# Normalising the first token tile by halves, with its square sums added on GpSimd and the early weight conversions spaced out

## The chip, the cores and the metric

The kernel runs on one core of a Trainium2 chip. The metric is the device time of one execution in microseconds (us). The engines are TensorE (PE in the profile, its weight loads PEld), VectorE (DVE), ScalarE (ACT), GpSimd (POOL) and SyncE (SP), which issues all the DMA transfers of this kernel.

## The reference

Three layers run one after another on 4 x 576 = 2304 tokens of width 512, all in float32.

```python
scores = q @ k.T / 8                              # 4 batches, 8 heads of 64, 576 positions
x = (scores * gamma[h] ** (i - j) * (j <= i)) @ v # retention
rms = sqrt(mean(x * x, axis=-1) + 1e-6)
xn = x / rms * rms_g
g = xn @ w_gate                                   # 512 -> 1536
y = (g * sigmoid(g) * (xn @ w_val)) @ w_out       # 1536 -> 512
out = relu(y @ w_in) ** 2 @ w_out2                # 512 -> 2048 -> 512
```

## The kernel before

**Layout.** Activations lie transposed in `X`, channels on the partitions (4 blocks of 128) and tokens along the row. Retention is done in 16 pairs (4 batches x 4 pairs of heads). `scores(n, half)` multiplies q by k for chunks of 128 positions and masks the product on VectorE, `state(n)` builds the state between chunks (`R`), `outputs(n, half)` forms the output and writes it to `X`, `scale_v(n)` scales the values on ScalarE. The loop for `n` runs `scores(n, 0)`, `outputs(n-1, 0)`, `state(n)`, `scores(n, 1)`, `outputs(n-1, 1)`.

**Weights.** A weight piece is 128 x 512 numbers of 8 bytes. It is loaded into one of three staging buffers (`load_piece`), and `convert_piece` turns it into a main part and a rest, both of the type that TensorE multiplies (`w[:, 0]`, `w[:, 1]`): three ScalarE and four VectorE instructions. Activations are split the same way (`split_x`, tiles `xh` and `xl`), and each product is made of three (`mm3`). `halves(k)` adds k to a counter; each 2 in it convert one piece, and each conversion loads the piece that lies `cv["ahead"]` further on. `LOAD_W` names the loops at whose start `ahead` grows by one, `CONVERT_ALONE` the loops of the first eight at whose end conversions stand.

**The first token tile.** Tokens 0 to 511 are complete after pair 3. They are normalised in two groups of 256 tokens during the next pairs, by steps listed in `NORMS` under (loop, half): "squares" (ScalarE squares, then two additions that fold 4 blocks into one), "roots" (TensorE sums over partitions into bank `ssq`, then a reciprocal root of two VectorE and twelve GpSimd instructions), "scale" (TensorE spreads the roots into bank `rms`, VectorE scales `X`) and "split" (`xh`, `xl`). From loop 8 on (`FIRST` is 7), 20 blocks of the second layer's first product (`glu_gate`, `glu_val`, 12 products each) run between the pairs: `block()`. Before loop 8, `keep_warm` issues products of zeros into a bank `junk`, one call at each half of a loop.

**Order.** TensorE's and SyncE's instructions run in the order of the program text. A planner orders VectorE, ScalarE and GpSimd by its own estimate of when inputs are there; `tc.high_priority()` around the steps of `NORMS` raises them in it. All queues run in order on the chip. `CONVERT_BEHIND[cv["phase"]]` can bind a conversion behind the last ScalarE ("a") and VectorE ("d") instruction that the text has issued; in phases 0 and 1 it is free, in 2 and 3 it is bound to both.

Of the kernel before, what the change touches and what calls it, by code (L numbers as in the profile page):

```python
# [11 lines left out]
ALU = mybir.AluOpType  # L12
PSUM = bass.MemoryType.PSUM

P = 128
# [15 lines left out]
GRP = 256  # L31
NGV = 2 * NF1
# [4 lines left out]
NWB = NF1 - NKEPT // 2 - NWC  # L37
FIRST = 7
WARM = (8, 6, 5, 5)
WARM_PAIR = (1, 1)  # L40
NORMS = {
    (4, 0): [("squares", 0)], (4, 1): [("squares", 1)], (5, 1): [("roots", (0, 1))],
    (7, 0): [("scale", 0), ("split", 0)], (7, 1): [("scale", 1), ("split", 1)],
    (9, 0): [("squares", 2)], (10, 0): [("roots", (2,))], (11, 0): [("scale", 2)],
}
LOAD_W = (4, 5, 6)
CONVERT_ALONE = {5: 2, 6: 2, 7: 4}
CONVERT_BEHIND = ("", "", "ad", "ad")
RSQRT_MAGIC = float(0x5F3759DF)
I32 = mybir.dt.int32  # L50
# [5 lines left out]
def retention_then_glu_then_relu2(ctx: ExitStack, tc: tile.TileContext, qk, kv, w1, w2, g, cmask, cvs, cgi, cgc, cid, out):  # L56
    nc = tc.nc
# [14 lines left out]
    def bank(tag, name):  # L72
        return psum.tile([P, 512], F32, tag=tag, name=name)
# [5 lines left out]
    ones = const.tile([P, 1], F32, name="ones")  # L79
# [12 lines left out]
    last_on = {}  # L92
    cv = {"load": 0, "done": 0, "half": 0, "lim": 0, "load_lim": NP1, "phase": 0, "ahead": 0}
# [14 lines left out]
    def convert():  # L108
        i = cv["done"]
        if i not in raws or i >= cv["lim"]:  # L110
            return False
        raw = raws.pop(i)
        with ExitStack() as behind:
            for e in CONVERT_BEHIND[cv["phase"]]:
                behind.enter_context(tc.issue_after(last_on[e].ins))
            convert_piece(i, raw)
        cv["done"] += 1
        return True
# [21 lines left out]
    def halves(k):  # L140
        cv["half"] += k
        while cv["half"] >= 2 and convert():
            cv["half"] -= 2
        cv["half"] = min(cv["half"], 2)

    def need(n):
        while cv["done"] < n:
            assert convert()


    aside = wa.tile([P, 2, 512], F32, tag="w", name="aside")
    ident, sums = aside[:, 0, :P], aside[:, 1].rearrange("p (i n) -> p i n", i=2)
    cols_ = aside[:, 0, P:P + 12].rearrange("p (k n) -> p k n", k=3)
# [4 lines left out]
    alone = {"on": True}  # L158
# [34 lines left out]
    def keep_warm(k, new=False):  # L193
        if new:
            junk["t"] = bank("G", f"junk{len(junk)}")
        for _ in range(k):
            nc.tensor.matmul(junk["t"][:, :P], zero, zero, start=True, stop=True)
# [102 lines left out]
    def roots(y, z, ms, sums, aside=False):  # L300

        last_on["d"] = nc.vector.tensor_scalar(
            out=ms, in0=sums, scalar1=1.0 / DM, scalar2=1e-6, op0=ALU.mult, op1=ALU.add
        )
        last_on["d"] = nc.vector.tensor_scalar(
            out=y.bitcast(I32), in0=ms.bitcast(I32), scalar1=-0.5, scalar2=RSQRT_MAGIC, op0=ALU.mult, op1=ALU.add
        )
        for _ in range(3):
            if aside:
                nc.gpsimd.tensor_tensor(out=z, in0=y, in1=y, op=ALU.mult)  # L310
                nc.gpsimd.tensor_tensor(out=z, in0=z, in1=ms, op=ALU.mult)
                nc.gpsimd.tensor_scalar(out=z, in0=z, scalar1=-0.5, scalar2=1.5, op0=ALU.mult, op1=ALU.add)
                nc.gpsimd.tensor_tensor(out=y, in0=y, in1=z, op=ALU.mult)
                continue
            for o, a, c, op0, b, op1 in (
                (z, y, -0.5, ALU.mult, y, ALU.mult), (z, z, 1.0, ALU.mult, ms, ALU.mult), (y, z, 1.5, ALU.add, y, ALU.mult),
            ):
                last_on["d"] = nc.vector.scalar_tensor_tensor(out=o, in0=a, scalar=c, in1=b, op0=op0, op1=op1)

    def scale_x(i, rb):  # L320
        ts = slice(i * GRP, i * GRP + GRP)
        for k in range(KC):
            last_on["d"] = nc.vector.scalar_tensor_tensor(
                out=X[:, k, ts], in0=X[:, k, ts], scalar=gsb[:, k:k + 1], in1=rb, op0=ALU.mult, op1=ALU.mult
            )
# [17 lines left out]
    def beside(what, i):  # L343
        nb = GRP // P
        if what == "squares":
            sq = wa.tile([P, KC, GRP], F32, tag="w", name=f"sq{i}")
            last_on["a"] = nc.scalar.activation(out=sq, in_=X[:, :, i * GRP:i * GRP + GRP], func=AF.Square)
            last_on["d"] = nc.vector.tensor_tensor(out=sq[:, 0:2], in0=sq[:, 0:2], in1=sq[:, 2:4], op=ALU.add)
            last_on["d"] = nc.vector.tensor_tensor(out=sums[:, i % 2], in0=sq[:, 0], in1=sq[:, 1], op=ALU.add)
        elif what == "roots":  # L350
            pb = bank("V", f"ssq{i[0]}")
            for j in range(nb * len(i)):
                nc.tensor.matmul(
                    pb[:, j:j + 1], sums[:, i[j // nb] % 2, j % nb * P:j % nb * P + P], ones, start=True, stop=True
                )
            y, z, ms = (cols_[:, k, :nb * len(i)] for k in range(3))
            roots(y, z, ms, pb[:, :nb * len(i)], aside=True)
        elif what == "scale":
            rb = bank("V", f"rms{i}")[:, :GRP]
            for j in range(nb):  # L360
                at = i % 2 * nb + j
                nc.tensor.matmul(
                    rb[:, j * P:j * P + P], cols_[:, 0, at:at + 1].to_broadcast([P, P]), ident, start=True, stop=True
                )
            scale_x(i, rb)
        else:
            split_x(i * GRP, GRP, i * GRP)
# [126 lines left out]
    for n in range(1, NPAIR + 1):  # L494
        mixed = n > FIRST
        if n in LOAD_W:
            cv["ahead"] += 1
            load_ahead(cv["done"])
        if n == FIRST + 1:
            alone["on"] = False  # L500
            cv["phase"] = 1
        if n < NPAIR:
            scores(n, 0)
        if mixed:
            block()
        else:
            keep_warm(WARM_PAIR[0], True)
        outputs(n - 1, 0)
        stages(n, 0)
        if n < NPAIR:  # L510
            state(n)
            if n == NPAIR - 1:
                att_kv.close()
                wpool["c"] = ctx.enter_context(tc.tile_pool(name="wc", bufs=NWC, side="right", reuse_waits="tile"))
                cv["lim"] = NGV + NWC
                cv["load_lim"] = NP1
                load_ahead(cv["done"])
        if mixed:
            block()
        else:  # L520
            keep_warm(WARM_PAIR[1])
        if n < NPAIR:
            scores(n, 1)
        outputs(n - 1, 1)
        stages(n, 1)
        scale_v(n + 1)
        halves(CONVERT_ALONE[n] if n in CONVERT_ALONE else 2 * mixed)
    assert points["done"] == len(blocks)
    att.close()
    cv["phase"] = 2  # L530
# [180 lines left out]
```

## Time and profile before

| | |
|---|---|
| runs, median (lowest to highest) | 965.57 us (965.51 to 967.13) |
| profiled execution, time | 966.28 us |
| profiled execution, span from first to last instruction | 964.5 us |
| TensorE busy | 938.8 us (97%) |
| VectorE busy | 493.7 us (51%) |
| ScalarE busy | 339.7 us (35%) |
| GpSimd busy | 23.0 us (2%) |
| mean granted TensorE clock | 0.989 of full |

Of the profiled time, 1.78 us lies outside the span. TensorE's 25.7 us without work and the granted clock by stage are what the change can touch; the other engines matter where TensorE waits for them.

### The profile page before, as it was taken

To read this page: it belongs to the slowest core of one execution; us is meant where nothing else is said; L and a number is where in the kernel's file an instruction comes from. 1 tells how busy PE (TensorE), PEld (TensorE's weight loads), DVE (VectorE), ACT (ScalarE), POOL (GpSimd) and SP (SyncE) were. 2 spreads that over 40 slices of the span, in tenths; PEclk is the share of its full clock that TensorE was granted. 3 is DMA by queue.
4 is the path that set the end of the run, shared out by engine and by line. 5 is a ranking of instruction groups with operands and counts; after the bars stand their busy time and mean duration, and the time that the engine had idled before them with its cause. 6 is when DMAs were issued, how large, how long until landed. Compare 5 with 4: busy or idle time off the path is not lost.

```text
span 964.5 us, 12744 instructions
## 1 busy us (share of the span) xinstructions
PE 938.8 (97%) x5248; PEld 782.9 (81%) x5248; DVE 493.7 (51%) x917; ACT 339.7 (35%) x606; POOL 23.0 (2%) x44
## 2 busy tenths in 40 slices
PE   9859999899999999999999999999999999999998
PEld 8747776799988888888888888888888888888897
DVE  3777887677655424442587786632224222322332
ACT  2544452555231113111455565432223222322332
POOL 0100100002010000000000000000000000000000
PEclk9969999999999999999999999999999999999999
DMA  8844653231000000000044423001001000100010
GB/s 291 291 146 147 225 185 109 65 111 44 1 1 1 23 1 1 22 22 1 13 141 131 131 95 103 22 1 45 0 1 45 1 1 1 43 1 1 1 45 22
DMA packets 22554, 60.92 MB, mean 63 GB/s; under 512 B 2656, under 2 KB 3936, under 8 KB 22496
## 3 DMA queue, kind: packets, MB, share of 16 engines
q1 hardware_dynamic: 22496, 60.11, 18.7%
q8 instruction: 41, 0.67, 0.3%
q14 instruction: 17, 0.14, 0.0%
HBM read 55.39 MB, written 4.72 MB: 62 GB/s over the span
## 4 chain that ended last, share of the span: by engine, by line
PE 91%; DMA 4%; DVE 3%; ACT 1%; issue 1%; SPq 0%; ACTq 0%; DVEq 0%
PE b L625 7%; PE pr L385 7%; PE pr L387 7%; PE pr L386 7%; PE b L626 7%; PE b L627 7%; PE a L385 5%; PE a L386 5%; PE a L387 5%; PE pv L385 5%; PE pv L387 5%; PE pv L386 5%; PE pg L385 5%; PE pg L386 5%; PE pg L387 5%; DMA raw<-in_w 3%
## 5 line engine op out<-in xcount | busy, mean ns | idle before, releaser
L614 DVE TENSOR_TENSOR X<-X 128x512 f32<-128x512 f32 (+1 forms) x80 | 51.1, 639 | 189.3 <-ACT X L613 188.3
L414 ACT ACTIVATE h<-X 128x512 fp32r<-128x512 f32 (+1 forms) x132 | 77.5, 587 | 160.6 <-DVE X L434 86.3
L415 DVE TENSOR_TENSOR h<-X,h 128x512 fp32r<-128x512 f32 (+1 forms) x132 | 84.4, 639 | 70.2 <-ACT h L414 69.0
L387 PE MATMUL pr<-xh,w 128*128 128x512 f32 (+1 forms) x320 | 117.7, 368 | 0.0
L386 PE MATMUL pr<-xl,w 128*128 128x512 f32 (+1 forms) x320 | 117.7, 368 | 0.0
L385 PE MATMUL pr<-xh,w 128*128 128x512 f32 (+1 forms) x320 | 117.6, 368 | 0.0
L613 ACT ACTIVATE X<-pr 128x512 f32<-128x512 f32 (+1 forms) x80 | 44.4, 555 | 194.0 <-PE pr L387 193.9
L625 PE MATMUL b<-w,h 128*128 128x512 f32 x288 | 112.4, 390 | 0.0
L626 PE MATMUL b<-w,h 128*128 128x512 f32 x288 | 112.2, 390 | 0.0
L627 PE MATMUL b<-w,h 128*128 128x512 f32 x288 | 112.0, 389 | 0.0
L385 PE MATMUL pg<-xh,w 128*128 128x512 f32 (+1 forms) x240 | 90.7, 378 | 7.1 <-ACT xh L372 6.6
L385 PE MATMUL pv<-xh,w 128*128 128x512 f32 (+1 forms) x240 | 90.7, 378 | 2.3 <-ACT w L136 2.3
L386 PE MATMUL pg<-xl,w 128*128 128x512 f32 (+1 forms) x240 | 89.6, 373 | 1.2 <-DVE xl L373 1.2
L387 PE MATMUL pg<-xh,w 128*128 128x512 f32 (+1 forms) x240 | 89.1, 371 | 0.0
L387 PE MATMUL pv<-xh,w 128*128 128x512 f32 (+1 forms) x240 | 88.6, 369 | 0.0
L386 PE MATMUL a<-h,w 128*128 128x512 f32 (+1 forms) x240 | 88.5, 369 | 0.0
L385 PE MATMUL a<-h,w 128*128 128x512 f32 (+1 forms) x240 | 88.5, 369 | 0.0
L387 PE MATMUL a<-h,w 128*128 128x512 f32 (+1 forms) x240 | 88.4, 368 | 0.0
L386 PE MATMUL pv<-xl,w 128*128 128x512 f32 (+1 forms) x240 | 88.4, 368 | 0.0
L425 ACT ACTIVATE X<-pg 128x512 f32<-128x512 f32 (+1 forms) x52 | 28.5, 548 | 117.3 <-PE pg L387 115.0
L426 DVE TENSOR_TENSOR X<-pg,X 128x512 f32<-128x512 f32 (+1 forms) x52 | 32.6, 627 | 72.2 <-ACT X L425 72.2
L386 PEld LDWEIGHTS pr<-xl,w 128*128 128x128 f32 x320 | 60.3, 188 | 10.6
(96 smaller groups left out, 1465.5 us busy)
## 6 DMA issues: line engine op xcount, KB each, us to landing
raw<-in_w SPq DMA_DIRECT2D x68, 512.0 KB, 3.8
X<-in_qk SPq DMA_DIRECT2D x11, 576.0 KB, 5.2
out<-o SPq DMA_DIRECT2D x18, 256.0 KB, 2.1
v<-in_kv SPq DMA_DIRECT2D x14, 320.0 KB, 3.8
k<-in_kv SPq DMA_DIRECT2D x14, 256.0 KB, 3.0
qk<-in_qk SPq DMA_DIRECT2D x4, 576.0 KB, 5.3
X<-in_kv SPq DMA_DIRECT2D x2, 320.0 KB, 5.2
X<-in_kv SPq DMA_DIRECT2D x2, 256.0 KB, 4.8
```

The costliest lines, as they stand in the source:

```text
L385: nc.tensor.matmul(dst, whi, xhi, start=start, stop=False, skip_group_check=True)
L386: nc.tensor.matmul(dst, whi, xlo, start=False, stop=False, skip_group_check=True)
L387: nc.tensor.matmul(dst, wlo, xhi, start=False, stop=stop, skip_group_check=True)
L414: last_on["a"] = nc.scalar.activation(out=h[:, 0, :n], in_=s, func=AF.Copy)
L415: last_on["d"] = nc.vector.tensor_tensor(out=h[:, 1, :n], in0=s, in1=h[:, 0, :n].bitcast(F32), op=ALU.subtract)
L425: last_on["a"] = nc.scalar.activation(out=s, in_=pg[:, :n], func=AF.Sigmoid)
L426: last_on["d"] = nc.vector.tensor_tensor(out=s, in0=pg[:, :n], in1=s, op=ALU.mult)
L613: last_on["a"] = nc.scalar.activation(out=s, in_=pg[:, :n], func=AF.Relu)
L614: last_on["d"] = nc.vector.tensor_tensor(out=s, in0=s, in1=s, op=ALU.mult)
L625: nc.tensor.matmul(a[m], hh, w[:, 0], start=f == 0, stop=False)
L626: nc.tensor.matmul(a[m], hh, w[:, 1], start=False, stop=False)
L627: nc.tensor.matmul(a[m], hl, w[:, 0], start=False, stop=f == NF2 - 1)
```

## The change

Seven edits:

- `NORMS`: "roots" is done for group 0 in loop 5, first half, and for group 1 in the second half (before: both at once in the second half). "scale" and "split" of group 0 move from loop 7, first half, to loop 6, second half; those of group 1 from loop 7, second half, to its first half.
- "squares": the two additions go from VectorE to GpSimd, for groups 0, 1 and 2.
- "roots" and "scale" use bank tag G before loop 8 (before: V).
- `WARM_PAIR`: the calls of `keep_warm` stay in loops 1 and 2 and go in loops 3 to 7.
- `LOAD_W` from (4, 5, 6) to (2, 3, 5), `CONVERT_ALONE` from one piece in loop 5, one in loop 6 and two in loop 7 to one each in loops 3, 4 and 7.
- Loop 8 gets phase 2 (conversions bound behind the last ScalarE and VectorE instruction); phase 1 begins with loop 9.
- `need(NGV)` after loop 16 converts what is left of the 24 pieces of the first two matrices there.

```diff
-WARM_PAIR = (1, 1)
+WARM_PAIR = {1: (1, 1), 2: (1, 1)}
 NORMS = {
-    (4, 0): [("squares", 0)], (4, 1): [("squares", 1)], (5, 1): [("roots", (0, 1))],
-    (7, 0): [("scale", 0), ("split", 0)], (7, 1): [("scale", 1), ("split", 1)],
-    (9, 0): [("squares", 2)], (10, 0): [("roots", (2,))], (11, 0): [("scale", 2)],
+    (4, 0): [("squares", 0)], (4, 1): [("squares", 1)], (5, 0): [("roots", 0)], (5, 1): [("roots", 1)],
+    (6, 1): [("scale", 0), ("split", 0)], (7, 0): [("scale", 1), ("split", 1)],
+    (9, 0): [("squares", 2)], (10, 0): [("roots", 2)], (11, 0): [("scale", 2)],
 }
-LOAD_W = (4, 5, 6)
-CONVERT_ALONE = {5: 2, 6: 2, 7: 4}
+LOAD_W = (2, 3, 5)
+CONVERT_ALONE = {3: 2, 4: 2, 7: 2}
...
-            last_on["d"] = nc.vector.tensor_tensor(out=sq[:, 0:2], in0=sq[:, 0:2], in1=sq[:, 2:4], op=ALU.add)
-            last_on["d"] = nc.vector.tensor_tensor(out=sums[:, i % 2], in0=sq[:, 0], in1=sq[:, 1], op=ALU.add)
+            nc.gpsimd.tensor_tensor(out=sq[:, 0:2], in0=sq[:, 0:2], in1=sq[:, 2:4], op=ALU.add)
+            nc.gpsimd.tensor_tensor(out=sums[:, i % 2], in0=sq[:, 0], in1=sq[:, 1], op=ALU.add)
         elif what == "roots":
-            pb = bank("V", f"ssq{i[0]}")
-            for j in range(nb * len(i)):
-                nc.tensor.matmul(
-                    pb[:, j:j + 1], sums[:, i[j // nb] % 2, j % nb * P:j % nb * P + P], ones, start=True, stop=True
-                )
-            y, z, ms = (cols_[:, k, :nb * len(i)] for k in range(3))
-            roots(y, z, ms, pb[:, :nb * len(i)], aside=True)
+            pb = bank("G" if alone["on"] else "V", f"ssq{i}")
+            for j in range(nb):
+                nc.tensor.matmul(pb[:, j:j + 1], sums[:, i % 2, j * P:j * P + P], ones, start=True, stop=True)
+            y, z, ms = (cols_[:, k, i % 2 * nb:i % 2 * nb + nb] for k in range(3))
+            roots(y, z, ms, pb[:, :nb], aside=True)
         elif what == "scale":
-            rb = bank("V", f"rms{i}")[:, :GRP]
+            rb = bank("G" if alone["on"] else "V", f"rms{i}")[:, :GRP]
...
         if n == FIRST + 1:
             alone["on"] = False
+            cv["phase"] = 2
+        if n == FIRST + 2:
             cv["phase"] = 1
...
-            keep_warm(WARM_PAIR[0], True)
+            keep_warm(WARM_PAIR.get(n, (0, 0))[0], n in WARM_PAIR)
...
-            keep_warm(WARM_PAIR[1])
+            keep_warm(WARM_PAIR.get(n, (0, 0))[1])
...
         halves(CONVERT_ALONE[n] if n in CONVERT_ALONE else 2 * mixed)
+    need(NGV)
     assert points["done"] == len(blocks)
```

## Rows read from the trace of the kernel before

**Rows 1.** Busy time by stretch: each engine's, then granted clock, DMA share, GB/s

```profile
22.20:68.00 45.80, 31.75 (x408) 26.01 (x404) 35.89 (x87) 22.10 (x44) 3.46 (x12) 0.84 0.71 240
32.00:48.00 16.00, 13.81 (x192) 11.07 (x188) 13.96 (x37) 10.00 (x19) 3.46 (x12) 1.00 0.86 289
...
76.60:160.00 83.40, 81.27 (x757) 63.63 (x756) 69.54 (x150) 40.01 (x76) 4.00 (x12) 1.00 0.58 192
140.00:160.00 20.00, 17.87 (x168) 13.75 (x166) 18.63 (x39) 10.25 (x19) 0.00 (x0) 1.00 0.49 154
160.00:180.00 20.00, 17.70 (x111) 13.77 (x110) 7.64 (x15) 5.14 (x9) 0.00 (x0) 1.00 0.06 19
200.00:600.00 400.00, 400.00 (x1921) 337.50 (x1920) 234.94 (x418) 147.44 (x252) 14.08 (x12) 1.00 0.15 47
```

**Rows 2.** What TensorE waited for: us in total, times, longest

```profile
PE pg L385 <- ACT xh L372: 6.6, 1, 6.6
PE junk L197 <- DVE xl L373: 3.4, 1, 3.4
...
PE pv L385 <- ACT w L136: 2.3, 1, 2.3
```

**Rows 3.** Busy time, two stretches around the fall of the clock

```profile
48.00:49.80 1.80, 0.00 (x0) 0.00 (x0) 1.80 (x5) 1.03 (x3) 0.00 (x0) 0.96 0.88 295
...
68.00:73.50 5.50, 5.21 (x11) 3.76 (x12) 2.64 (x7) 1.15 (x3) 0.00 (x0) 0.50 0.00 0
```

**Rows 4.** Timeline, 53 to 77 us: start, us, instruction, idle before

```profile
53.50 4.15 SPq L100 DMA_DIRECT2D raw<-in_w  x3
...
61.26 0.66 ACT L123 ACTIVATE u<-raw 128x512 f32<-128x512 f32 x1 [4.62 <-DMA raw<-in_w]
...
67.06 1.64 DVE L323 SCALAR_TENSOR_TENSOR X<-X,gsb,rms 128x256 f32<-128x256 f32 x4
...
68.03 0.80 PE L385 MATMUL pg<-xh,w 128*128 128x512 f32 x1 [6.62 <-ACT xh L372]
...
73.77 0.40 PE L385 MATMUL pv<-xh,w 128*128 128x512 f32 x1
...
75.21 1.88 DVE L137 TENSOR_TENSOR w<-u,w 128x512 fp32r<-128x512 f32 x3
...
76.62 0.44 PE L283 MATMUL o<-X,R 64*64 64x128 f32 x4
```

**Rows 5.** Chain that ended last, in loop 3: start, us, what

```profile
22.95 0.42 PE junk L197 x2
```

**Rows 6.** Timeline, the first products of loops 3 and 4

```profile
22.23 0.72 PE L230 MATMUL s<-X 64*128 64x128 f32 x8
...
27.29 0.71 PE L230 MATMUL s<-X 64*128 64x128 f32 x8
```

**Rows 7.** VectorE's groups, 20 to 76 us: count, busy us, mean ns

```profile
L128 DVE SCALAR_TENSOR_TENSOR raw<-raw 128x512 int32<-128x512 int32 x8 | 5.4, 688 | 0.1
...
L125 DVE TENSOR_SCALAR u<-u 128x512 f32<-128x512 f32 x7 | 2.9, 418 | 6.5 <-ACT u L123 6.5
...
L348 DVE TENSOR_TENSOR sq<-sq 128x512 f32<-128x512 f32 x2 | 1.4, 692 | 1.4 <-ACT sq L347 1.4
L349 DVE TENSOR_TENSOR aside<-sq 128x256 f32<-128x256 f32 x2 | 0.8, 411 | 0.0
```

**Rows 8.** GpSimd's group of a whole-kernel addition of squares

```profile
L332 POOL TENSOR_TENSOR sq<-sq 128x512 f32<-128x512 f32 x6 | 8.6, 1431 | 187.6 <-ACT sq L331 187.6
```

**Rows 9.** Timeline of GpSimd and VectorE where they overlap

```profile
42.73 0.90 POOL L310 TENSOR_TENSOR aside<-aside 128x4 f32<-128x4 f32 x1 [32.48 <-DVE aside L305]
...
46.90 0.20 POOL L313 TENSOR_TENSOR aside<-aside 128x4 f32<-128x4 f32 x1
...
232.44 1.59 POOL L332 TENSOR_TENSOR sq<-sq 128x512 f32<-128x512 f32 x1 [6.79 <-ACT sq L331]
...
232.80 1.78 DVE L128 SCALAR_TENSOR_TENSOR raw<-raw 128x512 int32<-128x512 int32 x1
```

## The prediction

> **What bounds the kernel now.** I read the busy time by stretch first. From 200 to 600 us TensorE has work in all 400.00 us at full clock [rows 1], so whatever is gained earlier arrives whole at the end. The reader is to see next that the loss lies ahead of that: between 22.2 us, where loop 3 begins, and 68.0 us TensorE is busy 31.75 of 45.80 us. What TensorE waited for says why: one wait of 6.6 us for `xh`, one of 3.4 us for `xl`, both in the normalisation of the first tile, and later one of 2.3 us for a converted weight [rows 2].
>
> The timeline shows the mechanism of the longest. Three weight pieces were issued at 53.50 us. ScalarE's next conversion stood idle for 4.62 us until one landed at 61.26 us; VectorE's part of it stood ahead of the scaling of group 1, which began at 67.06 us; the first block product followed at 68.03 us [rows 4]. So the planner had put free conversions ahead of the urgent scaling, and in-order queues made TensorE wait for a transfer that nobody needed yet.
>
> The waits also cost the clock. It stood at 1.00 of full (2.4 GHz) from 32 to 48 us [rows 1], was still 0.96 in the 1.80 us to 49.8 in which TensorE did nothing, and 0.50 (the 1.2 GHz level) while the first block ran, which took 5.5 us [rows 3]; the same twelve products at full clock took 76.62 - 73.77 = 2.85 us with the change of operands behind them [rows 4].
>
> **The first block's new start.** I call it T; before, it is 68.03 us. Three floors and a chain decide it.
>
> TensorE's floor: a pair took 27.29 - 22.23 = 5.06 us [rows 6]. Two calls of zeros in it cost 2 x 0.42 = 0.84 us [rows 5]; without them a pair takes 4.2 us. From loop 3's start five pairs are 21.0 us; the two sums over partitions, two spreads and one more scoring, a few small products each, I bound by nothing and by one further pair. T is at least 43.2 to 47.4, under VectorE's floor either way.
>
> VectorE's floor: 35.89 us of work lay between 22.2 and 68.0 us [rows 1]. Out of it go two groups' additions, 2 x (0.69 + 0.41) = 2.2 us [rows 7]. A conversion costs 0.34 us for its short step and 0.60 for each of three long ones (three of them took 1.88 us in a row [rows 4], so each adds 0.60 and the last 0.08): 2.14 us. Before, four were complete by 68 us and three more were done but for the last step, which is the row of three at 75.21: 4 x 2.14 + 3 x 1.54 = 13.2 us. The change asks for three, 6.4 us, so 6.8 goes. Into it come what lay behind 68.0 us before: half of group 1's four scalings (0.8 of 1.64 [rows 4]) and its four rests at 0.41 less 0.08 of overlap [rows 7], 2.2 us together; and one more preparation of roots, two tiny steps under 0.41 each, put at 0.3. That is 35.9 - 2.2 - 6.8 + 2.5 = 29.4 us. The third conversion is needed only by the third block and may come behind: 27.3 us as the low bound, T = 49.5.
>
> GpSimd's chain: the additions cost there 1.43 us for the large one [rows 8] and, by half the elements, at least 0.72 for the small one, and the twelve steps of a root took 47.1 - 42.7 = 4.4 us [rows 9]. Two groups in a row are 2 x (2.15 + 4.4) = 13.1 us. Group 0 is complete with the first half of loop 4, which begins at 27.3 [rows 6], so by some 30 us; the last root is there by about 43, ahead of VectorE's floor. So splitting the roots lengthens GpSimd's chain by a root, and that stays hidden; without this cover TensorE would wait in order at the spread for the excess, with `state(7)` behind it.
>
> GpSimd's additions aren't free to VectorE. Where one of 1.59 us ran, a VectorE step that otherwise takes 0.69 us took 1.78 [rows 7, 9]: 1.1 us lost against 0.69 saved, and about 0.5 against 0.41 for the small addition, as an estimate by size. Where VectorE is idle beside them the loss is nothing. The bounds are 0 and 2 x 1.6 = 3.2 us; I take 1.5, since VectorE was busy 13.96 of 16.00 us just there. The Trainium skill, "GPSIMD Engine Reference", section "Key points", says that GpSimd shares its SBUF interfaces with VectorE and contends with its instructions that have two SBUF inputs, and that elementwise work is about half as fast there. The trace agrees on both (1.43 against 0.69 us, and the step of 1.78). By the rule alone this edit would be a loss; it is the smallest edit here.
>
> So VectorE has 29.4 + 1.5 - 2.1 = 28.8 us of work ahead of T. Its fill in the like stretch was 13.96/16.00 = 0.87 [rows 1]: 33.1 us, T = 55.3. Between the full fill and this, near the second because its row is the nearest, I choose **T = 54.5**. First term: 68.0 - 54.5 = 13.5 us. Second: if TensorE is at full clock by then, the first block saves 5.5 - 2.85 = 2.65 us. Together 16.2 us, measured at the end of the second block.
>
> **The rest.** The zeros' 10 x 0.42 = 4.2 us lie in the same stretch, where VectorE is the bound, and give nothing beyond T; without VectorE's cover they would be worth 4.2. The earlier loads (a piece in loops 2 and 3) push key and value loads back on SyncE's one queue; DMA is at 0.86 there [rows 1], one piece of 0.52 MB at 289 GB/s is 1.8 us. Values are loaded two pairs ahead, 8.4 us or more; so this is hidden, and its bound is 2 x 1.8 us on T. The change of banks is nothing: the zeros leave G free.
>
> The mixed stretch, 76.6 to 160 us, gives something back. By then before had converted seven pieces, after the change three: four conversions, 8.5 us of VectorE, move into a stretch where it is busy 69.54 of 83.40 us, less 1.1 for the third group's additions. That makes 77 of 83.4, 92%. The last 20 us of that stretch show what this fill costs: at 18.63 of 20 TensorE lost 2.13 us [rows 1]. At that rate over the whole stretch it would lose 8.9 instead of 2.13, so 6.8 more is the upper bound and nothing the lower. VectorE is busy only 7.64 of 20 us from 160 to 180 [rows 1], where some can go. I take +3.0.
>
> `need(NGV)` converts the 24th piece in that quiet stretch: the wait of 2.3 us [rows 2] goes: -2.3. The bound on the other side is 0, if the wait passes to the split of the next tile. Binding loop 8's conversions costs no work; pieces 3 and 4 start behind the second block and the end of loop 8, and are needed by the fourth and fifth block, over half a pair later. A conversion is three ScalarE steps like the one of 0.66 us [rows 4] and 2.14 us of VectorE, 4.1 in all; eight mixed pairs took some 83.4 us, half of one 5.2. So it is hidden, by a margin of one.
>
> Sum: -13.5 - 2.65 + 3.0 - 2.3 = -15.5 us. Profiled time 966.28 - 15.5 = 950.8; the runs' median lies 0.7 below the profiled execution, so I say 950.5, between the two.
>
> **Rivals.**
>
> *The clock falls (11%).* With 24 us of work in a stretch of 32, TensorE has more gaps than in the 13.81 of 16.00 at which the clock stayed at 1.00 [rows 1], and it falls as it did after 48.0 [rows 3]; the zeros that go had filled such gaps. For it speaks that fall; against it, that the wait ahead of it was a single long one. If loops 5 to 7 run at half clock, 15 us of products become 5.5/2.85 = 1.93 times as long, 14 us more on TensorE's floor: T = 57 to 61, 60 taken, and the first block keeps its 5.5. Sum -8.0 + 3.0 - 2.3 = -7.3: 959. The Trainium skill, "TensorE: Matmul & The Clock Gate", section "Why this matters for your kernels", speaks for it: it advises against idle gaps between bursts of products.
>
> *VectorE bounds the mixed stretch (15%).* All four later conversions come out as TensorE's time: -16.2 + 8.5 - 2.3 = -10.0: 956.
>
> *The stall comes back (slower, 6%).* If the planner puts a conversion whose load is late ahead of group 1's scaling, as at 61.26 us, T stays at 68 with the clock down, and the four missing conversions still come later: +8.5 - 2.3 = +6.2: 972.5. It decides as soon as T passes 62. For it speaks that the planner did just that; against it, that the third piece is now loaded four loops ahead of its place and loop 8's are bound.
>
> *The change doesn't do what it says (4%).* T lands near 62 and the gain is eaten: within 2 us of 966.
>
> **Chances.** My forecast 64%, with its own range 943 (T = 49.5, nothing given back: -18.5 - 2.65 - 2.3) to 955. Range 942 to 960: it takes in VectorE's and most of the clock's case, and leaves out about 2 in 10. A change of 0.2% is about the least that can be told here from none. Faster 0.90, same 0.03, slower 0.07.
>
> **What would show it.** Right: no TensorE wait over 2 us for `xh` or `xl`; the first `pg` between 49 and 57 us at full clock; four records of zeros fewer in each of loops 3 to 7; no wait for `w` near 160; the gain whole from there on. Wrong: granted clock near 0.5 before the first block; ScalarE idle for `raw` ahead of an `xh`; VectorE over 95% full in the mixed stretch with TensorE waiting for `X` or `w`.

## The result and the profile after

The changed kernel takes 952.78 us (median of 4 runs, 951.69 to 953.63) against 965.54 us; the ratio is 0.987, 95% interval 0.9846 to 0.9894, a gain of 12.8 us. The profiled execution took 952.30 us with a span of 950.5 us, 14.0 less than before. TensorE is busy for 936.6 us instead of 938.8, so 11.8 us of the 14.0 are idle time that went. The forecast was 950.5, range 942 to 960.

The stretches, which answer to [rows 1] and [rows 3] (each engine's busy time, then TensorE's granted clock, DMA share, GB/s):

```profile
22.20:56.20 34.00, 30.32 (x396) 25.38 (x390) 28.17 (x69) 16.03 (x34) 9.31 (x28) 0.80 0.72 243
32.00:48.00 16.00, 13.15 (x120) 11.01 (x122) 12.92 (x29) 7.48 (x15) 9.31 (x28) 0.57 0.62 217
34.00:47.70 13.70, 12.13 (x108) 10.26 (x108) 10.92 (x25) 6.41 (x11) 9.12 (x27) 0.50 0.58 201
140.00:160.00 20.00, 19.42 (x157) 15.05 (x156) 13.75 (x30) 6.49 (x14) 0.00 (x0) 1.00 0.33 107
166.00:176.00 10.00, 8.38 (x50) 7.58 (x50) 7.64 (x17) 5.51 (x14) 0.00 (x0) 0.83 0.27 95
200.00:600.00 400.00, 400.00 (x1888) 336.00 (x1887) 230.69 (x410) 145.40 (x248) 13.47 (x12) 1.00 0.14 44
```

From 200 to 600 us nothing has changed: TensorE is full, and the gain made earlier arrives whole. Ahead of the first block it is now busy for 30.32 of 34.00 us, where it was 31.75 of 45.80 [rows 1]. But from 34 to 47.7 us the clock stands at 0.50 (1.2 GHz), where it was 1.00 before [rows 1]. TensorE's waits up to 205 us (us in total, times, longest), which answer to [rows 2]:

```profile
PE pg L384 <- DVE xl L371: 2.4, 3, 1.2
PE s L230 <- DVE ret L240: 1.5, 1, 1.5
PE ssq L353 <- POOL aside L349: 1.5, 1, 1.5
PE u L259 <- DVE X L295: 1.3, 1, 1.3
```

The three long waits of [rows 2], 6.6, 3.4 and 2.3 us, are gone, and nothing above 1.5 us stands in their place. Where the clock fell is read from the chain of work that ended last (first four lines: start, us, what) and the timeline behind it:

```profile
22.60 7.80 DMA raw<-in_w
...
30.43 0.68 ACT u L123
...
31.72 0.69 DVE raw L128
32.41 0.60 DVE ret L240
```

```profile
33.07 0.71 PE L230 MATMUL s<-X 64*128 64x128 f32 x8 [1.53 <-DVE ret L240]
...
35.12 1.27 POOL L348 TENSOR_TENSOR sq<-sq 128x512 f32<-128x512 f32 x1 [24.70 <-ACT sq L347]
...
35.64 1.03 DVE L125 TENSOR_SCALAR u<-u 128x512 f32<-128x512 f32 x1 [0.21 <-ACT u L123]
...
37.31 1.01 PE L353 MATMUL ssq<-ones,aside 128*128 128x1 f32 x4 [1.47 <-POOL aside L349]
...
38.24 1.27 POOL L348 TENSOR_TENSOR sq<-sq 128x512 f32<-128x512 f32 x1 [0.99 <-ACT sq L347]
...
38.33 1.73 DVE L131 SCALAR_TENSOR_TENSOR u<-u,raw 128x512 int32<-128x512 int32 x1
...
54.19 1.65 DVE L323 SCALAR_TENSOR_TENSOR X<-X,gsb,rms 128x256 f32<-128x256 f32 x4
...
56.22 0.49 PE L383 MATMUL pg<-xh,w 128*128 128x512 f32 x1
...
57.53 0.50 PE L384 MATMUL pg<-xl,w 128*128 128x512 f32 x1 [0.82 <-DVE xl L371]
...
63.08 0.69 DVE L432 TENSOR_TENSOR kept<-pv,kept 128x512 f32<-128x512 f32 x1 [0.30 <-PE pv L385]
```

The second piece of weights, now asked for two loops earlier, took 7.80 us to land. ScalarE's conversion waited for it, VectorE's part of that conversion stood ahead of the mask of loop 4, and TensorE waited 1.53 us for the mask. From 34 us, 1 us behind this wait, the clock stood at 0.50; the wait of 1.47 us at the sums of squares came when it was down already. It was back at 1.00 well before the first block product, which came at 56.22 us instead of 68.03 [rows 4].

Five places mark how the 14.0 us came about: the first block product (T), VectorE's last step of the second block, its first step of a tile named `late` (close to the end of the mixed stretch), its last one of this tile, and the span.

| us | before | after | difference of this part | said |
|---|---|---|---|---|
| T | 68.03 | 56.22 | -11.8 | -13.5 |
| second block | 77.01 | 63.08 | -2.1 | -2.65 |
| first `late` step | 172.70 | 159.41 | +0.6 | +3.0 |
| last `late` step | 183.21 | 167.42 | -2.5 | -2.3 |
| span | 964.5 | 950.5 | +1.8 | 0 |

### The profile page after: what moved, and what is told of

Its sections match the earlier page's. It is cut to its first block, busy times and chain, and to the rows that moved or that the text cites. A ratio compares the mean times of both kernels' runs of the same rounds, so it can differ in the third digit from the quotient of the medians.

```text
span 950.5 us, 12727 instructions
## 1 busy us (share of the span) xinstructions
PE 936.6 (99%) x5228; PEld 782.2 (82%) x5228; DVE 491.5 (52%) x913; ACT 339.2 (36%) x606; POOL 31.8 (3%) x62
## 4 chain that ended last, share of the span: by engine, by line
PE 89%; DMA 5%; DVE 4%; ACT 1%; issue 1%; SPq 0%; POOL 0%; ACTq 0%; DVEq 0%
PE b L626 7%; PE pr L384 7%; PE pr L383 7%; PE pr L385 7%; PE b L627 7%; PE b L628 7%; PE a L383 5%; PE a L384 5%; PE a L385 5%; PE pg L383 5%; PE pg L384 5%; PE pg L385 5%; PE pv L383 5%; PE pv L385 4%; PE pv L384 4%; DMA raw<-in_w 4%
## 5 line engine op out<-in xcount | busy, mean ns | idle before, releaser
L383 PEld LDWEIGHTS pr<-xh,w 128*128 128x128 f32 x320 | 60.3, 188 | 10.7
L385 PEld LDWEIGHTS pr<-xh,w 128*128 128x128 f32 x320 | 60.3, 188 | 10.1
```

Of the source, the lines that this page charges most:

```text
L383: nc.tensor.matmul(dst, whi, xhi, start=start, stop=False, skip_group_check=True)
L385: nc.tensor.matmul(dst, wlo, xhi, start=False, stop=stop, skip_group_check=True)
```

## The experiments

Each edit is against the changed kernel unless it says otherwise. Ratios are to the kernel before, from runs on the same chip; the other columns are the five places of the table above, each from one profiled execution (in run 7 VectorE's step of the second block was itself late, and is left out).

| | ratio, 95% interval | T | second block | first `late` | last `late` | span |
|---|---|---|---|---|---|---|
| after | 0.987, 0.9846 to 0.9894 | 56.22 | 63.08 | 159.41 | 167.42 | 950.5 |
| 1 normalisation alone | 1.0001, 0.9979 to 1.0023 | 66.60 | 77.54 | 170.27 | 182.09 | 962.9 |
| 2 loads and conversions back | 0.9901, 0.9872 to 0.993 | 53.92 | 66.71 | 166.01 | 174.01 | 955.5 |
| 3 early conversions bound | 0.9851, 0.9818 to 0.9884 | 51.85 | 61.14 | 158.87 | 166.88 | 949.5 |
| 4 zeros back | 0.9961, 0.994 to 0.9981 | 64.86 | 70.82 | 170.74 | 178.75 | 961.8 |
| 5 zeros back in loops 3, 4, 6 | 0.9903, 0.9877 to 0.9929 | 57.61 | 64.93 | 165.61 | 173.62 | 956.7 |
| 6 before without zeros | 0.9958, 0.9943 to 0.9973 | 62.83 | 71.01 | 165.49 | 177.25 | 958.6 |
| 7 loop 8 free | 0.9852, 0.9829 to 0.9876 | 55.78 | - | 158.68 | 166.69 | 950.1 |
| 8 additions on VectorE | 0.9839, 0.9814 to 0.9864 | 55.38 | 62.32 | 159.67 | 167.67 | 949.2 |
| 9 roots later | 0.9876, 0.9855 to 0.9897 | 54.25 | 61.53 | 159.76 | 167.77 | 950.8 |
| 10 same, additions on VectorE | 0.9877, 0.9857 to 0.9896 | 53.83 | 62.06 | 159.80 | 167.80 | 950.8 |
| 11 same, conversions bound | 0.9877, 0.9855 to 0.9898 | 56.25 | 63.36 | 160.45 | 168.46 | 951.5 |
| 12 without `need(NGV)` | 0.9912, 0.9893 to 0.9931 | 52.03 | 59.26 | 157.04 | 171.07 | 952.2 |

**1. The normalisation's new places alone.** The kernel before, with the new `NORMS`, the roots by group and the banks; everything else as before.

```diff
-    (4, 0): [("squares", 0)], (4, 1): [("squares", 1)], (5, 1): [("roots", (0, 1))],
-    (7, 0): [("scale", 0), ("split", 0)], (7, 1): [("scale", 1), ("split", 1)],
+    (4, 0): [("squares", 0)], (4, 1): [("squares", 1)], (5, 0): [("roots", 0)], (5, 1): [("roots", 1)],
+    (6, 1): [("scale", 0), ("split", 0)], (7, 0): [("scale", 1), ("split", 1)],
```

> The kernel before with one part of the change alone: the roots by group, the earlier places of roots, scale and split, and their bank G; additions on VectorE, zeros, loads, conversions and the end of loop 16 as before. Theory N (the normalisation's earlier place is what takes the long stall away): the waits of 6.6 and 3.4 us for xh and xl go, the first block starts before 60 us, and the time is 952 to 957 us. Rival B (the stall comes from free conversions whose loads are late, wherever the normalisation stands): a conversion still stands ahead of a scaling, the first block starts after 63 us, and the time is 961 us or more.

It gained nothing: 967.2 us, ratio 1.0001. Yet the wait of 6.6 us for `xh`, on which the prediction rested its story, is gone. Five of its waits (the others are of 2.1 us and less):

```profile
PE junk L197 <- DVE xl L371: 4.8, 1, 4.8
PE pv L383 <- ACT w L136: 2.3, 1, 2.3
...
PE u L259 <- issue: 1.8, 1, 1.8
...
PE junk L197 <- DVE aside L302: 1.2, 1, 1.2
...
PE u L259 <- DVE aside L302: 1.0, 1, 1.0
```

All but the second of these stand at the products of zeros, or at the state products that share bank tag G with them. The code says why. The operand of the zeros is a corner of the tile that the split writes, `zero = xl[:, 0, :P]`, so a product of zeros behind `split(0)` in the text waits for that write; and `junk` holds one of the two buffers of tag G through both halves of a loop, so that `u` gets the one whose reader VectorE has not finished. The 3.4 us of [rows 2], read in the prediction as a wait of the normalisation, is a wait of the zeros. Neither theory written for this run had that; runs 4 to 6 bear on it. Ahead of T TensorE's idle time falls from 14.1 to 9.1 us, but the same products keep it busy for 35.3 us instead of 31.8, since more of them ran at the lower clock; and the second block takes the 1.4 us of T back.

**2. Loads and conversions back.**

```diff
-LOAD_W = (2, 3, 5)
-CONVERT_ALONE = {3: 2, 4: 2, 7: 2}
+LOAD_W = (4, 5, 6)
+CONVERT_ALONE = {5: 2, 6: 2, 7: 4}
```

> The changed kernel with LOAD_W and CONVERT_ALONE as before. Theory L (loops 4 to 6 of the changed kernel lost time because weight loads moved into a stretch where DMA was already full, so that piece 1 landed 7.8 us after its issue, its conversion held up a mask and the squares, and TensorE's two waits of 1.5 us brought the clock down for 13.7 us): those waits go, the clock is 1.00 from 34 to 47 us, the first block starts before 54 us; time 946 to 950 us unless the later conversions stall something else. Rival Z (the clock fell because the zeros are gone): the clock still falls to 0.5 in loops 5 and 6, and the time stays at 952 us or rises.

957.35 us, ratio 0.9901: by the ratios 3.0 us more than the changed kernel, with intervals that overlap. Beside run 3, which keeps the new loads and was measured with it on one chip, its six times (955.25 to 959.6) all lie above the four there (951.31 to 953.74). Of theory L, T before 54 us came true (53.92). Its quiet start did not: TensorE waits 3.15 us at `ssq`, and the clock is 0.75 from 34 to 47.7 us. The theory's own reservation, later conversions that stall something else, did come true: the second product of the same block waits, and the timeline shows what for (start, us, instruction, idle before):

```profile
55.04 0.68 DVE L131 SCALAR_TENSOR_TENSOR u<-u,raw 128x512 int32<-128x512 int32 x1
...
55.64 0.68 DVE L137 TENSOR_TENSOR w<-u,w 128x512 fp32r<-128x512 f32 x1
...
57.24 0.41 DVE L371 TENSOR_TENSOR xl<-X,xh 128x256 fp32r<-128x256 f32 x1
...
57.70 0.79 PE L384 MATMUL pg<-xl,w 128*128 128x512 f32 x1 [3.31 <-DVE xl L371]
```

On VectorE two steps of a conversion and a mask stand between the rests of group 0 and the first rest of group 1, at 57.24 us, for which TensorE waits. So the mechanism of [rows 4], free conversions in the way of the urgent split, does exist, and the new places of the loads remove it.

**3. The early conversions bound,** behind the last instruction of the text.

```diff
-CONVERT_BEHIND = ("", "", "ad", "ad")
+CONVERT_BEHIND = ("ad", "", "ad", "ad")
```

> The changed kernel with the conversions ahead of loop 8 bound behind the last ScalarE and VectorE instructions of the text, as those of loop 8 are; loads as in the changed kernel. Theory L: the conversion of piece 1 no longer stands ahead of loop 4's mask and squares, TensorE's waits of 1.5 us go or fall under 0.7, the clock stays at 1.00, the first block starts at 50 to 53 us, time 946 to 950 us. Rival Z: the clock falls all the same, first block at 55 to 57 us, time 951 to 954 us.

952.7 us, ratio 0.9851. The first block comes 4.4 us earlier (51.85), as theory L had it, though not by its reason: a wait of 2.78 us at `ssq` is still there, the clock falls to 0.50 behind it, and is back after 3.5 us. The time is the one of rival Z. Of the 4.4 us, 1.9 are left at the second block and 0.5 at the first `late` step. Where the last part of it goes is told under run 12.

**4. The zeros back** in loops 3 to 7.

```diff
-WARM_PAIR = {1: (1, 1), 2: (1, 1)}
+WARM_PAIR = {n: (1, 1) for n in range(1, 8)}
```

> The changed kernel with the products of zeros in loops 3 to 7 again. Rival Z: the clock stays at 1.00 through loops 5 and 6, the first block starts 2 to 5 us earlier than at 56.2, time 947 to 950 us. Theory L: the zeros wait in TensorE's queue behind the same two waits, the clock falls all the same or a little later, and up to 4.2 us of zeros are added where TensorE has no slack; time 952 to 957 us.

962.02 us, ratio 0.9961: 8.8 us of the 12.8 are gone by the ratios, with 4.2 us of added products. That is above the ranges of both theories. T is 64.86. The timeline of TensorE, with the scaling on VectorE in between, and three stretches (columns as above; the last one is all that lies ahead of T):

```profile
38.89 1.12 PE L259 MATMUL u<-v,k 128*64 128x64 f32 x16 [3.01 <-DVE aside L302]
...
53.45 0.49 PE L197 MATMUL junk<-xl 128*128 128x128 f32 x2 [2.04 <-DVE xl L371]
...
56.29 1.66 DVE L323 SCALAR_TENSOR_TENSOR X<-X,gsb,rms 128x256 f32<-128x256 f32 x4 [0.73 <-PE rms L360]
...
58.05 1.12 PE L259 MATMUL u<-v,k 128*64 128x64 f32 x16 [1.80 <-issue]
```

```profile
38.00:42.00 4.00, 3.11 (x31) 2.55 (x33) 3.88 (x9) 1.59 (x4) 3.25 (x5) 0.50 0.39 121
...
54.00:62.00 8.00, 6.20 (x55) 4.87 (x56) 5.15 (x15) 1.81 (x5) 0.00 (x0) 0.53 0.20 55
...
22.20:64.80 42.60, 35.34 (x416) 29.04 (x412) 31.38 (x77) 17.41 (x37) 9.37 (x28) 0.80 0.65 219
```

The state products wait 3.01 us for the reader of the sums (`aside`, L302, which reads bank `ssq`), the zeros of loop 7 wait 2.04 us for the split, and the state products of loop 7 wait 1.80 us; that one the trace calls "issue", but it ends 0.1 us behind VectorE's last reading of bank `rms`, at 57.95 us. The clock is near half behind the first and behind the other two. VectorE is busy for only 31.38 of the 42.60 us ahead of T, a fill of 0.74, so here it isn't the bound. Against the changed kernel (30.32 of 34.00 us) TensorE has 5.0 us more busy time ahead of T and 3.6 us more idle time. The zeros' own products are all of the first: eight of the ten calls at 0.42 us and two at half clock, at twice that, make 5.0.

**5. The zeros back in loops 3, 4 and 6 only,** where no split and no sum is next to them.

```diff
-WARM_PAIR = {1: (1, 1), 2: (1, 1)}
+WARM_PAIR = {n: (1, 1) for n in (1, 2, 3, 4, 6)}
```

> The changed kernel with the products of zeros again in loops 3, 4 and 6, but not in 5 and 7. Theory W (zeros cost by what they wait for: in loop 5 they hold a bank of tag G that the sums need, in loop 7 they also read a corner of xl that the split of group 0 writes; the products themselves cost 0.84 us a loop at most): no wait of a junk product for xl, none of u over 1 us for the sums' bank, first block at 56 to 59 us, time 952 to 956 us. Rival T (the zeros cost TensorE's time and order wherever they stand): three of five loops' worth of the 9.5 us that all five cost, so 957 to 960 us.

955.54 us, ratio 0.9903, as the theory of the waits had it (952 to 956). Neither the wait of the zeros for the split nor that of the state products for L302 appears. Of the 8.8 us that the zeros cost, 5.6 belong to loops 5 and 7 (0.9961 against 0.9903, intervals apart), whose products are 4 x 0.42 = 1.7 us. The other 3.2 belong to the other three loops, which add 6 x 0.42 = 2.5 us of products [rows 5]; their interval overlaps that of the changed kernel.

**6. The kernel before, without the zeros** of loops 3 to 7 (the calls get a count of 0 there).

```diff
-            keep_warm(WARM_PAIR[0], True)
+            keep_warm(WARM_PAIR[0] * (n < 3), n < 3)
...
-            keep_warm(WARM_PAIR[1])
+            keep_warm(WARM_PAIR[1] * (n < 3))
```

> The kernel before without the products of zeros in loops 3 to 7, nothing else changed. Theory W: the wait of 3.4 us of a junk product for xl goes, the long wait for xh behind a late weight load stays in kind, the first block starts 3 to 6 us before 68.0, time 959 to 963 us. Rival D (the late load bounds the first block, and zeros only fill): the wait for xh grows by what the other loses, first block at 66 us or later, time 964 to 967 us. Rival Z (the clock falls earlier without zeros): first block after 68 us, time over 967 us.

961.2 us, ratio 0.9958, again within the theory of the waits. Its two longest waits:

```profile
PE pg L385 <- ACT xh L372: 5.8, 1, 5.8
PE pv L385 <- ACT w L136: 2.3, 1, 2.3
```

The wait on `junk` is gone, the one for `xh` stays. Of the 5.2 us by which T is earlier, 3.4 are busy time of TensorE and 1.8 idle time:

```profile
22.20:62.80 40.60, 28.35 (x397) 23.80 (x396) 33.89 (x85) 19.86 (x41) 3.47 (x12) 0.88 0.78 274
```

So the parts of the change belong together: the zeros' removal alone is worth 4.1 us, everything but that 3.8 (run 4), all of it 12.8. The new places alone gave nothing (run 1); they and the removal of the zeros without the rest were not run.

**7. Loop 8 free.**

```diff
-            cv["phase"] = 2
-        if n == FIRST + 2:
             cv["phase"] = 1
```

> The changed kernel with free conversions in loop 8 (phase 1 there, as before the change). Theory B (binding loop 8 keeps conversions whose loads are late from standing ahead of group 1's scaling and split): ScalarE or VectorE waits for raw ahead of the last xl, a TensorE wait for xh or xl of 3 us or more comes back, time 956 to 962 us. Rival: loop 8's loads are early enough by now, no such wait, time 951 to 954 us.

950.82 us, ratio 0.9852, no worse than the changed kernel. Binding loop 8's conversions is not what keeps the stall away.

**8. The additions of squares on VectorE.**

```diff
-            nc.gpsimd.tensor_tensor(out=sq[:, 0:2], in0=sq[:, 0:2], in1=sq[:, 2:4], op=ALU.add)
-            nc.gpsimd.tensor_tensor(out=sums[:, i % 2], in0=sq[:, 0], in1=sq[:, 1], op=ALU.add)
+            last_on["d"] = nc.vector.tensor_tensor(out=sq[:, 0:2], in0=sq[:, 0:2], in1=sq[:, 2:4], op=ALU.add)
+            last_on["d"] = nc.vector.tensor_tensor(out=sums[:, i % 2], in0=sq[:, 0], in1=sq[:, 1], op=ALU.add)
```

> The changed kernel with the additions of squares on VectorE again. Theory G (on GpSimd they are slower and stretch VectorE's steps beside them, and the sums of group 0 come later: TensorE waited 1.5 us for them): the wait of ssq shrinks under 0.7 us, the clock falls later or not at all, time 948 to 952 us. Rival V (VectorE is so full there that each addition costs more on it): first block later than 56.2 us, time 953 to 957 us.

949.3 us, ratio 0.9839 against 0.987 with overlapping intervals; runs 9 and 10, the same comparison with the roots elsewhere, give 0.9876 and 0.9877. So no gain from GpSimd's additions is seen, and by run 8 alone they would cost 3.0 us, which the intervals leave open. Theory G had the time but not the way: TensorE's wait at `ssq` did not shrink, it is 3.4 us.

**9 to 11. The roots half a loop later,** alone, with the additions on VectorE, and with the early conversions bound as well.

```diff
-    (4, 0): [("squares", 0)], (4, 1): [("squares", 1)], (5, 0): [("roots", 0)], (5, 1): [("roots", 1)],
+    (4, 0): [("squares", 0)], (4, 1): [("squares", 1)], (5, 1): [("roots", 0)], (6, 0): [("roots", 1)],
```

> The changed kernel with the root steps half a loop later: group 0's in the second half of loop 5, group 1's in the first half of loop 6. In the changed kernel TensorE waits in order for the sums of squares (1.5 us at the product ssq), and the granted clock falls to half at 34 us right behind it and stays down to 47.7. Theory Q (the sums are asked for too early and the gap costs the clock): the wait at ssq goes, the clock stays at 1.00 from 34 us to the first block, the first block product comes at 51 to 53 us instead of 56.2, and VectorE takes the second block's value product at 58 to 60 us instead of 63.1; time 946 to 950. Rival G (given back): the first block comes earlier by those us, but the mixed stretch from 63 to 166 us loses them again, since VectorE's conversions then are late; time 950 to 953. Rival R (the roots are on the path): GpSimd's 4 to 6 us for each root now end later than TensorE's spread wants them, the wait moves from ssq to rms with 2 us or more, and the time is 953 or above.

> The kernel with the roots half a loop later, and the additions of squares on VectorE as before. Theory Q: as with the roots later alone, 946 to 950; putting the additions back was worth 0 to 3 us with the early roots, and with the wait at ssq gone it should be worth 0 to 1, since what hid behind the wait is no longer on the path. Rival G: 949 to 952, the place of the additions and of the roots both without effect because the mixed stretch sets the end.

> The kernel with the roots later and the additions on VectorE, and the free conversions of the first eight loops bound behind the last instruction of the text on ScalarE and VectorE. Bound conversions brought the first block from 56.2 to 51.9 us in the changed kernel and gave 2 us less than that at the end. Theory Q: first block at 49 to 51 us, time 944 to 948. Rival G: first block there as well, but the mixed stretch loses what was won; time 948 to 952.

953.0, 952.6 and 952.6 us: all three stand where the changed kernel does, and theory Q fell. The wait for GpSimd at `ssq` did go in run 9, but one like it is there at the same time, and the clock falls all the same (timeline of TensorE, then stretches):

```profile
36.26 0.77 PE L283 MATMUL o<-X,R 64*64 64x128 f32 x12 [1.45 <-DVE X L295]
```

```profile
34.00:38.00 4.00, 2.55 (x39) 2.16 (x40) 2.74 (x6) 2.99 (x5) 2.07 (x3) 1.00 1.00 384
38.00:42.00 4.00, 3.35 (x24) 2.41 (x24) 4.00 (x10) 1.66 (x5) 2.22 (x2) 0.51 0.85 315
```

What TensorE waits for there is VectorE's output of the pair. It stood behind a conversion step that waited for ScalarE, which waited for a weight piece:

```profile
34.57 0.66 ACT L123 ACTIVATE u<-raw 128x512 f32<-128x512 f32 x1 [1.20 <-DMA raw<-in_w]
...
35.26 0.54 DVE L125 TENSOR_SCALAR u<-u 128x512 f32<-128x512 f32 x1 [1.51 <-ACT u L123]
...
35.73 0.48 DVE L295 TENSOR_TENSOR X<-o,gi 128x320 f32<-128x320 f32 x1
```

So in run 9 a late piece stands behind the gap, as in the changed kernel. And the lead that is won (T at 54.25 and 53.83 in runs 9 and 10) is given back by the first `late` step, as rival G had it. No version tried here is measurably better than the changed kernel.

**12. Without `need(NGV)`.**

> The changed kernel without the conversion of the last pieces behind loop 16. Theory of the prediction: TensorE's wait of about 2.3 us for a converted weight, which stood before at the value product near 177 us and is gone in the changed kernel, comes back, and the time is 954 to 956. Rival: the wait is taken by the split of the next tile or was never on the path; the time stays at 952 to 953.5.

956.12 us, ratio 0.9912: by the ratios 4.1 us slower than the changed kernel, by the medians 3.3, and just above the 954 to 956 of the prediction's theory. The wait comes back, at another product and twice as long (waits, then TensorE's timeline):

```profile
PE pg L383 <- ACT w L136: 5.0, 2, 4.6
```

```profile
163.67 0.62 PE L383 MATMUL pg<-xh,w 128*128 128x512 f32 x1 [4.58 <-ACT w L136]
```

This run shows two more things. VectorE's and ScalarE's instructions stand in the same order as in the changed kernel to past 100 us, and yet T is 52.03 instead of 56.22: ScalarE began on the weight piece at 29.31 instead of 30.43, the mask was in time, the wait of 1.53 us isn't there, and the clock is 0.88 from 34 to 47.7 us instead of 0.50. The stretch ahead of T, to be set beside the one of the changed kernel at the top:

```profile
22.20:52.00 29.80, 26.66 (x396) 22.37 (x393) 27.94 (x69) 16.02 (x36) 9.28 (x28) 0.94 0.84 286
```

The same 396 records of products kept TensorE busy for 26.66 us instead of 30.32, so 3.7 of the 4.2 us are the clock's. The two programs differ only behind loop 16. So T can move by 4 us between executions, and the T of single profiles above can't be compared closer than that; 64.86 and more (runs 1 and 4) lie outside.

The end of the runs moves far less, and the stretch from 128 to 142 us shows a part of the reason. The changed kernel, run 3 and run 12:

```profile
128.00:142.00 14.00, 13.42 (x128) 10.37 (x128) 14.00 (x30) 9.64 (x18) 0.00 (x0) 1.00 0.48 147
```

```profile
128.00:142.00 14.00, 11.87 (x125) 9.30 (x124) 14.00 (x30) 9.27 (x17) 0.00 (x0) 1.00 0.46 143
```

```profile
128.00:142.00 14.00, 12.22 (x105) 9.54 (x105) 14.00 (x30) 7.72 (x15) 0.00 (x0) 1.00 0.55 166
```

VectorE is busy for all 14.00 us in each of them: the conversions are made up here. Whoever comes early waits for it: 0.58 us for `X` at 140.90 us in the changed kernel, 1.49 us in run 3 and 1.48 in run 12 at the same product. TensorE is idle for 0.58, 2.13 and 1.78 us in this stretch, and between the second block and the first `late` step runs 3 and 12 give back 1.4 and 1.5 us of their lead. The other part of run 3's lead, 2.4 us, went between T and the second block, where TensorE waited 0.97 us for `xl` and 1.55 us for `R`. T anywhere from 51.85 to 56.25 ends in a span of 949.2 to 951.5 us in runs 3 and 7 to 11.

## Why the prediction was right, and where its steps were not

The number and the direction held. The size of the terms held better than the reasons for them.

**The zeros: the step that failed.** "The zeros' 10 x 0.42 = 4.2 us lie in the same stretch, where VectorE is the bound, and give nothing beyond T"; without that cover the prediction priced them at 4.2. They are worth 8.8 us in the changed kernel (run 4) and 4.1 in the one before (run 6). VectorE was not the bound that was to cover them: its fill is 0.83 ahead of the new T and 0.74 in run 4, while TensorE is busy for 30.32 of 34.00 us. So their own time counted, 5.0 of the 8.6 us by which T is later in run 4. The other 3.6 are idle time, and run 5 shows that it hangs on where they stand: in order, behind a split whose tile holds their operand and on a bank that the sums, the spread and the state need, with waits of 3.01, 2.04 and 1.80 us. The row that told it was on record, and was read as the normalisation's own [rows 2]. "The change of banks is nothing: the zeros leave G free" is right only in this pair: with the zeros there, the banks bring waits of their own (runs 1 and 4).

**The stall of [rows 4]** was described rightly, and was not the bound alone. Run 1 moves the scaling out of its way, the wait for `xh` goes, and nothing is won at the end: the zeros wait next, 4.8 us, and more products run at the lower clock. Run 6 takes the zeros away, and `xh` stays.

**T by VectorE's floor.** The 28.8 us of work forecast ahead of T are 28.17 in the profile; the fill is 28.17 / 34.00 = 0.83 for the 0.87 taken, so T is 56.2 instead of 54.5. In run 12 the same work, 27.94 us, fits in 29.80, a fill of 0.94. So VectorE's work is much the same and the fill is what differs, by 3.7 us of TensorE's busy time at the lower clock. That the work came so near is in part luck: all three conversions lie ahead of T, where the third, 2.1 us, was put behind it, and in exchange four of the eight rests (1.3 us) and a mask with its output come behind.

**The earlier loads** were called hidden, with a bound of 3.6 us. They aren't: a piece took 7.80 us to land, and the mask and TensorE behind it waited 1.53 us. Still their new places pay, by run 2 some 3.0 us with overlapping intervals, and its timeline shows the conversions in the split that they keep out; the prediction gave them nothing.

**The clock.** The rival of the falling clock came true in its mechanism and not in its price. It fell at 34 us, as the prediction had feared for loops 5 to 7, but was back at 1.00 before T, so the first two blocks gave their 2.1 us (2.65 forecast). What the fall and the late load cost together can be read from run 12, which had less of both: 4.2 us of T, 3.7 of them by the clock. Of such a lead 2.4 us are left at the first `late` step in run 12, and 0.5 in run 3. The Trainium skill, "TensorE: Matmul & The Clock Gate", section "Why this matters for your kernels", advises against idle gaps between bursts of products. By that, taking zeros out should hurt. Here it did not: the zeros could not fill the gaps, since they or the products beside them waited, and the longest gap of run 4, 3.01 us at 38.89, is about twice any in the changed kernel. Nor is it by the clock that the zeros cost time, for its mean ahead of T is 0.80 in both; and without zeros there are gaps as long in runs 2 and 8, 3.15 and 3.38 us at `ssq`.

**The additions on GpSimd.** The price on VectorE was as sized: beside GpSimd's 1.27 us at 38.24 a step of 0.69 took 1.73, and one of 0.42 took 1.03 at 35.64. The sum of both, 1.65 us, is near the 1.5 taken. The effect on the end is none that can be measured (runs 8 to 10). The Trainium skill, "GPSIMD Engine Reference", section "Key points", has the contention and the slower elementwise rate; the rows agree, and by its rule the edit is a loss, which run 8 leaves possible.

**The mixed stretch** gave back 0.6 us, at the lower part of the 0 to 6.8 given, and not the 3.0 taken. But the mechanism is there at the margin: VectorE full from 128 to 142 us, and 1.4 to 1.9 us of a lead lost between the second block and the first `late` step (runs 3, 9, 10 and 12). By that a still better T is not likely to have brought the 943 that the forecast's own range began with; it was not tried.

**`need(NGV)`** was worth 2.5 us in the markers, 2.3 said, and 4.1 by the ratio of run 12: without it a wait of 4.58 us comes in place of the 2.3 [rows 2]. **Binding loop 8** costs nothing, as said, and brings nothing (run 7).

**The signs named** came as said for the right case: no wait over 1.2 us for `xl` and none for `xh`, T between 49 and 57 us with the clock at 1.00, no wait for `w` near 160, the gain whole from 200 us on but for 1.8 us. Two of the wrong case were there as well, the clock at 0.50 ahead of the first block and VectorE full in part of the mixed stretch, and they took back less than was feared.

**Not foreseen:** 1.8 us lost between the last `late` step and the end. There are two waits for `xl` of the next tokens, 0.37 and 1.25 us at 167.6 and 169.4, and a clock of 0.83 from 166 to 176. In run 8 the same part is as long as before, with the same two waits. The clock alone isn't it: in runs 7 and 9 it is 1.00 from 166 to 176 us, and the part is as long as in the changed kernel or longer (783.4 and 783.0 us, against 783.1). What decides was not tried.

**Open:** why the mixed stretch is 3.0 to 4.4 us longer in runs 2, 4 and 5 than in the changed kernel (99.3, 99.9 and 100.7 us from the second block to the first `late` step, against 96.3). In runs 2, 4 and 5 the clock is 0.91 from 84 to 104 us and 1.00 in the changed kernel, which can't account for all of it. The 3.2 us in run 5 and the 3.0 in run 2 rest on intervals that overlap and on these five places; the steps to them are not shown.

## What to carry to other kernels

Products that only keep an engine awake cost their own time wherever that engine has no slack, 5.0 of 8.6 us here, and more where they can wait. So read each wait in their name as a cost of theirs, not of the tile that they happen to read; an operand that nobody writes and a bank that nobody else needs should take the waits away, which was not tried here. Two faults that stand one behind the other in an in-order queue hide each other: removing the first alone showed nothing (run 1), removing the second alone a third of the gain (run 6). Once an early stretch is mended, look for the next full engine downstream: of run 3's further lead of 4.4 us at T, 0.5 was left 107 us later, and 1.4 of what went was lost where VectorE was at 14.00 of 14.00.

## What the runs showed of the chip that was not expected

- Two executions, of programs that differ only behind loop 16, with the same order of instructions on VectorE and ScalarE up to past 100 us differed by 4.2 us in T. They part at a weight piece on whose landing ScalarE began at 29.31 or 30.43 us, with the DMA share near 1 (0.96 from 22 to 32 us in both), and the granted clock of the next 14 us was 0.88 or 0.50.
- Waits of 1.53, 0.31 and 1.47 us between 31.5 and 37.3 us stood around the fall of the clock, the first two ahead of it, and it was then 0.50 from 34 to 47.7 us, over 12.13 us of products.
- A VectorE step with one large input (L125, 0.42 us) took 1.03 us beside a GpSimd addition of 1.27 us, not only those with two.
